# A chunked state recurrence and a wave mixer on one core: each engine's order by a list scheduler in the kernel

## The chip, the cores and the metric

One core of a Trainium2 chip. Its engines run side by side, each in the order of its own queue: TensorE (PE; matmuls, with their weight loads as PEld), VectorE (DVE), ScalarE (ACT), GpSimd (POOL) and SyncE (SP, which only issues DMAs here). TensorE writes to PSUM, which has eight banks. The metric is the device time of a run in microseconds; the profile gives the span from the first to the last instruction of one execution.

## What is computed

Four batches, eight heads, 768 steps, 40 numbers a head. First a recurrence over time for each head, then a mixer over each batch:

```python
for t in range(S):
    y[:, :, t] = np.einsum('bhd,bhde->bhe', rt, state)
    Sa = np.einsum('bhde,bhe->bhd', state, at)
    state_decay = state * wt[:, :, None, :] - np.einsum('bhd,bhe->bhde', Sa, bt)
    state = state_decay + np.einsum('bhd,bhe->bhde', vt, kt)
...
theta = x @ w_theta
zr, zi = x * np.cos(theta), x * np.sin(theta)
u = x + np.einsum('ts,bsd->btd', w_tok_r, zr) + np.einsum('ts,bsd->btd', w_tok_i, zi)
out = u + np.maximum(u @ w_ch, 0.0)
```

Here x is y with the heads side by side, 320 numbers a step.

## The kernel before

The 768 steps are cut into six chunks of 128, so there are 24 tiles (four batches of six), each with 128 steps on the partitions and 320 columns. Tile i is worked on in these steps, which are functions of the kernel:

- load: six DMAs of SyncE bring w, k, b, a, r and v into four sets of raw buffers.
- prep_ln, prep_csi, prep_cse: the log of w (lw, ScalarE), two prefix sums of it as matmuls with triangular matrices, and an exp of each (invW and Wi, two ScalarE instructions). GpSimd multiplies k, b and a by them (kb, ah), and prep_rv casts r and v (rv).
- tr_kb, tr_a, tr_rv: transposes on TensorE against the identity, and copies of the transposed blocks out of PSUM (kbT by VectorE, aT by ScalarE, rvT by whichever evac names).
- sc_psiphi, ev_phi, sc_lams: four sets of score matmuls a tile, 64 rows each, and four masks on VectorE (psi, phi, lamv, lamu). Each set fills two banks.
- rec_x0 gives nx (ScalarE, with its sign turned), rec_nu the solve: nx is brought back through a matmul with the identity, and eight matmuls on phi are added. rec_gt makes the next state gt, rec_gd its transpose.
- out_nut, out_y, out_xt: the read-out y, which VectorE scales into x, and the transpose of x.
- moe_theta, moe_sines, moe_z: theta by three matmuls, its cosine and sine for three tiles at once (ScalarE has to change its function table before and after), and the products zr and zi on GpSimd.
- moe_y, moe_ut, moe_ch: a mixer row of a finished batch, that is twelve matmuls of 320 columns with the token weights, u, its transpose, three matmuls with the channel weights, and the store. wtok_load and wtok_trans bring and turn the token weights, a block of two loads and twelve transposes for each of six; a row needs all six chunks of its batch.

The order around all this is written by hand: one loop over tiles in which solve i stands with the preparation of tiles i + 1 to i + 3, out_y(i - 1) and the mixer rows of rows_at: one row in each of the iterations 9 to 20, two in 21 to 23, and the last batch's six behind the loop. PSUM is two pairs of banks for scores (ps_sc) and four single banks for the rest (ps_sm), handed out in turn. The calls that tc.keep_in_program_order marks keep their place on their engine.

Of the kernel before, what the change touches and what calls it, by code (L numbers as in the profile page):

```python
# [14 lines left out]
LN_EXP = "natural_log_exp_and_others"  # L15


@with_exitstack
def kernel(
# [14 lines left out]
    nc = tc.nc  # L34
# [5 lines left out]
    NT = NCH  # L40
    assert (B, H, S, D) == (4, 8, 768, 40)

    consts = ctx.enter_context(tc.tile_pool(name="consts", bufs=1))
    ident = consts.tile([128, 128], BF16, name="ident")
    make_identity(nc, ident)
    mask_p = consts.tile([128, 1, 128], BF16, name="mask_p")
    make_upper_triangular(nc, mask_p[:, 0, :], 1.0, diag=False)
    mask_n = consts.tile([128, 1, 128], BF16, name="mask_n")
    make_upper_triangular(nc, mask_n[:, 0, :], -1.0, diag=False)
    ntri_inc = consts.tile([128, 128], BF16, name="ntri_inc")  # L50
    make_upper_triangular(nc, ntri_inc, -1.0, diag=True)
# [10 lines left out]
    NB = 4  # L62

    def padded(name, shape, n, pads):
        ts = [consts.tile(shape, BF16, name=f"{name}_{i}") for i in range(n)]
        for i, t in enumerate(ts):
            to_zero.append((i, pads(t)))
        return ts

    to_zero = []  # L70

    def last24(t):
        return t[:, :, D:64] if len(t.shape) == 3 else t[:, :, :, D:64]

    lw_t = padded("lw", [128, H, 64], 2, last24)
    ah_t = padded("ah", [128, H, 64], 2, last24)
    kb_t = padded("kb", [128, 2, H, 64], NB, last24)
    rv_t = padded("rv", [128, 2, H, 64], NB, last24)
    nu_t = padded("nu", [128, H, 64], 2, last24)
    gt_t = padded("gt", [128, G, 2, 64], 2, last24)  # L80
    x_t = padded("x", [128, 3 * 128], 2 * NCH, lambda t: t[:, DM:])
    u_t = padded("u", [128, 3 * 128], 3, lambda t: t[:, DM:])
    for i, t in sorted(to_zero, key=lambda e: e[0]):
        nc.vector.memset(t, 0.0)

    raw = ctx.enter_context(tc.tile_pool(name="raw", bufs=4))
    exps = ctx.enter_context(tc.tile_pool(name="exps", bufs=4))
    trs = ctx.enter_context(tc.tile_pool(name="trs", bufs=3))
    scs = ctx.enter_context(tc.tile_pool(name="scs", bufs=2))
    sml = ctx.enter_context(tc.tile_pool(name="sml", bufs=2))  # L90
    xp = ctx.enter_context(tc.tile_pool(name="xp", bufs=2))
    mw = ctx.enter_context(tc.tile_pool(name="mw", bufs=1))
    mk = ctx.enter_context(tc.tile_pool(name="mk", bufs=2))
    mk1 = ctx.enter_context(tc.tile_pool(name="mk1", bufs=1))
    ps_sc = ctx.enter_context(tc.tile_pool(name="ps_sc", bufs=2, space=PSUM))
# [544 lines left out]
```

## Time and profile before

| | |
|---|---|
| three timed runs | 240.96, 242.19, 242.77 us |
| median | 242.19 us |
| span of the profiled execution | 239.3 us |
| busy: TensorE, VectorE | 205.4, 188.4 us |
| busy: ScalarE, GpSimd | 156.6, 119.2 us |

No separate time is given for the profiled execution; its span stands 2.9 us below the median of the runs, which also take in what lies around the span. TensorE's matmuls overlap, so a piece's duration is longer than the time by which it holds the next one back; that is read from the starts.

### The profile page before, as it was taken

What the parts mean: (1) busy time and instruction counts of PE and PEld (TensorE: products, weight loads), DVE (VectorE), ACT (ScalarE), POOL (GpSimd) and SP (SyncE); (2) the same over time, 40 slices, a digit from 0 to 9 for tenths busy, and PEclk for the clock granted to TensorE, in tenths of its full rate; (3) what the DMA queues carried; (4) which work ended last, traced back from release to release, by engine and by line L of the source; (5) the groups of instructions that cost most, each with busy time, mean ns of one, the idle gap of its engine ahead of it and who ended that gap; (6) DMA issues with size and microseconds to landing.
All of it is one profiled execution on the core that took longest, in us unless ns stands there. A gap on an engine that the chain in (4) does not pass through costs nothing.

```text
span 239.3 us, 8103 instructions
## 1 busy us (share of the span) xinstructions
PE 205.4 (86%) x3368; PEld 161.6 (68%) x3368; DVE 188.4 (79%) x290; ACT 156.6 (65%) x300; POOL 119.2 (50%) x184
## 2 busy tenths in 40 slices
PE   2679698957877999979999999999999998889982
PEld 1467577746655787767787787777777877666740
DVE  7558698895979798988899798979898869645062
ACT  4466577799469956867678785987698648325230
POOL 3009654666957693618753771657464730704100
PEclk9999999999999999999999999999999999999997
DMA  7999999999999999998899999948000000111013
GB/s 125 184 182 146 177 177 152 176 159 189 176 168 183 194 171 160 175 188 145 156 188 179 183 184 167 183 69 151 30 32 4 30 27 3 55 58 55 3 55 110
DMA packets 155684, 30.81 MB, mean 129 GB/s; under 512 B 150400, under 2 KB 155648, under 8 KB 155648
## 3 DMA queue, kind: packets, MB, share of 16 engines
q1 hardware_dynamic: 153216, 27.54, 62.9%
q0 software_dynamic: 2432, 2.77, 8.1%
q8 instruction: 26, 0.43, 0.8%
q14 instruction: 10, 0.08, 0.1%
HBM read 29.13 MB, written 3.93 MB: 138 GB/s over the span
## 4 chain that ended last, share of the span: by engine, by line
PE 50%; ACT 17%; DMA 12%; DVE 11%; issue 7%; POOL 1%; SPq 1%; DVEq 0%; ACTq 0%
PE sm L469 12%; PE sm L196 9%; DMA raw_w<-in_w_dram 9%; PE sc L228 8%; PE sm L424 5%; ACT cs L459 4%; DVE lamu L236 4%; DVE lamv L236 2%; ACT L459 2%; PE sc L469 2%; PE sm L363 2%; ACT lw L139 2%; ACT rvT L104 2%; PE sm L376 2%; DMA raw_a<-in_a_dram 2%
## 5 line engine op out<-in xcount | busy, mean ns | idle before, releaser
L168 POOL TENSOR_TENSOR kb<-raw_kb,invW 128x320 bf16<-128x320 f32 x44 | 37.1, 865 | 69.4 <-ACT invW L163 66.7
L236 DVE TENSOR_TENSOR lamv<-sc,mask_p 128x1024 bf16<-128x1024 f32 x24 | 29.4, 1224 | 12.0 <-PE sc L228 12.0
L469 PE MATMUL sm<-zr,wtok_r 128*128 128x320 bf16 x120 | 33.1, 299 | 0.6 <-DVE gt L324 0.6
L236 DVE TENSOR_TENSOR psi<-sc,mask_p 128x1024 bf16<-128x1024 f32 x24 | 29.3, 1223 | 5.1 <-PE sc L228 4.7
L469 PE MATMUL sm<-zi,wtok_i 128*128 128x320 bf16 x120 | 33.1, 299 | 0.0
L447 POOL TENSOR_TENSOR zr<-cs,x 128x320 bf16<-128x320 f32 x22 | 17.8, 811 | 27.4 <-ACT cs L459 27.3
L236 DVE TENSOR_TENSOR lamu<-sc,mask_p 128x1024 bf16<-128x1024 f32 x24 | 29.2, 1215 | 0.3 <-PE sc L228 0.3
L236 DVE TENSOR_TENSOR phi<-sc,mask_n 128x1024 bf16<-128x1024 f32 x24 | 29.1, 1215 | 0.0
L438 ACT COPY th<-sm 128x320 f32<-128x320 f32 x24 | 10.2, 426 | 18.3 <-PE sm L424 18.2
L345 ACT COPY nuT<-sm 128x512 bf16<-128x512 bf16 x24 | 14.1, 587 | 10.6 <-PE sm L196 10.6
L447 POOL TENSOR_TENSOR zi<-cs,x 128x320 bf16<-128x320 f32 x24 | 19.0, 794 | 3.4 <-ACT cs L459 2.8
L190 POOL TENSOR_TENSOR ah<-raw_a,Wi 128x320 bf16<-128x320 f32 x22 | 19.0, 864 | 0.0
L104 ACT COPY rvT<-sm 128x1024 bf16<-128x1024 bf16 x17 | 17.2, 1014 | 2.3 <-PE sm L196 2.3
L149 POOL CAST rv<-raw_rv 128x320 bf16<-128x320 f32 x44 | 18.6, 451 | 0.0
L477 DVE TENSOR_TENSOR u<-sm,x 128x320 bf16<-128x320 f32 x20 | 9.8, 490 | 10.7 <-PE sm L469 10.7
L469 PEld LDWEIGHTS <-wtok_i 128*128 128x128 bf16 x144 | 14.1, 98 | 6.2 <-issue 0.8
L469 PEld LDWEIGHTS <-wtok_r 128*128 128x128 bf16 x144 | 14.1, 98 | 6.0 <-issue 0.8
L196 PE MATMUL sm<-ident,kb 128*128 128x128 bf16 x192 | 15.7, 227 | 2.5 <-ACT nx L287 1.0
L207 DVE COPY kbT<-sm 128x1024 bf16<-128x1024 bf16 x24 | 16.4, 682 | 1.8 <-PE sm L196 1.8
L196 PE MATMUL sm<-ident,rv 128*128 128x128 bf16 x192 | 15.6, 226 | 1.5 <-ACT invW L163 0.8
L360 PE MATMUL sm<-kb,lamv 128*128 128x40 bf16 x192 | 16.7, 180 | 0.0
L228 PE MATMUL sc<-aT,kbT 64*128 64x128 bf16 x384 | 15.7, 225 | 0.7 <-ACT aT L214 0.7
(111 smaller groups left out, 598.9 us busy)
## 6 DMA issues: line engine op xcount, KB each, us to landing
raw_w<-in_w_dram SPq DMA_DIRECT2D x24, 160.0 KB, 4.1
raw_kb<-in_k_dram SPq DMA_DIRECT2D x24, 160.0 KB, 3.9
raw_kb<-in_b_dram SPq DMA_DIRECT2D x24, 160.0 KB, 4.0
raw_a<-in_a_dram SPq DMA_DIRECT2D x24, 160.0 KB, 3.9
raw_rv<-in_r_dram SPq DMA_DIRECT2D x24, 160.0 KB, 3.8
raw_rv<-in_v_dram SPq DMA_DIRECT2D x24, 160.0 KB, 4.2
out_dram<-oo SPq DMA_DIRECT2D x24, 160.0 KB, 1.8
wtok_row_r<-in_moe_w_tok_r_dram POOLq DMA_DIRECT2D x6, 192.0 KB, 4.2
```

The costliest lines, as they stand in the source:

```text
L104: nc.scalar.copy(out=out, in_=in_)
L149: on_pool(nc.gpsimd.tensor_copy(out=q.rvb[:, j, :, 0:D], in_=q.rv[:, j]))
L168: on_pool((nc.vector if i < 2 else nc.gpsimd).tensor_tensor(out=q.kbh[:, j, :, 0:D], in0=q.kb[:, j], in1=q.invW[:, 0], op=ALU.mult), i)
L190: on_pool((nc.vector if i < 2 else nc.gpsimd).tensor_tensor(out=q.ah[:, :, 0:D], in0=q.a, in1=q.Wi[:, 0:DM].rearrange("p (h d) -> p h d", ...
L196: nc.tensor.transpose(out=dst[:, g * 128:(g + 1) * 128], in_=src[:, 2 * g:2 * g + 2, :].rearrange("p a b -> p (a b)"), identity=ident)
L207: nc.vector.tensor_copy(out=q.kbT.rearrange("p a b -> p (a b)"), in_=pt)
L228: nc.tensor.matmul(P[:, p, g, :], lhsT=lhs[rows(p), g * 128:(g + 1) * 128], rhs=rhs[rows(p), g * 128:(g + 1) * 128], start=True, stop=True)
L236: nc.vector.tensor_tensor(out=s.rearrange("p a b c -> p (a b) c"), in0=P.rearrange("p a b c -> p (a b) c"), in1=mask.to_broadcast([128, 2 ...
L360: nc.tensor.matmul(o, lhsT=q.lamv[:, p, g, :], rhs=q.kbh[:, 0, h, 0:D], start=first, stop=False, skip_group_check=True)
L447: tc.keep_in_program_order(eng.tensor_tensor(out=zs[bi][c][:, js[m]], in0=cs[:, c, m], in1=tiles[bi * NCH + js[m]].x, op=ALU.mult))
L459: tc.keep_in_program_order(nc.scalar.activation(out=cs[:, c, 0:n], in_=ths[bi][:, j0:j0 + n], func=AF.Sin, bias=(pi2_col[:, :], 0.0)[c]))
L469: nc.tensor.matmul(yp, lhsT=wtok[nm][:, sb, j * 128:(j + 1) * 128], rhs=z[:, sb], start=start and n == 0, stop=stop and n == 2 * len(sbs) - 1)
```

## The change

All steps are now described to a planner (class Plan): each with its engine, what it reads and writes, a cost in ns and a priority from a table (OFF, in us, plus PERIOD times the tile). Plan.order simulates the engines, DMA queues and PSUM banks with these costs, and at each point gives an engine the step with the lowest priority, plus a price for time that it would wait. The steps are then issued in the planned order, with no reordering behind it, in the banks that the plan chose: four banks as two pairs, four single. Beside the order these things change:

- The solve adds phi's matmuls to the bank in which x0 still stands. nx is copied without the sign, which moves to the copy of nu; the matmul with the identity is gone.
- Both prefix sums go to one pair of banks, and one exp reads both; four masks and this exp now share the two pairs. off_diag is added to the first sum too, eight columns more.
- Copies of transposed blocks read the 16-bit pairs as 32-bit words, half as many elements, all on ScalarE (those of the token weights stay on VectorE).
- A mixer row is planned in six chunks of two matmuls. Its first chunk takes a bank only if more than two single banks are free (one in the last batch).
- The sines of a batch come as two groups of three, as before, and the last batch's as three, two and one. The last tile's sines read PSUM.

```diff
-    rows_at = {}
-    for s in range(NCH + 3, 3 * NCH + 3):
-        rows_at[s] = [divmod(s - NCH - 3, NCH)]
...
+OFF = dict(load=-32.72, ln=-14.21, cs=-14.27, exp=-12.91, kb=-24.2, ah=-17.45, rv=-8.81,
...
+PERIOD = 7.54
...
+        def find(o):
+            n = o.new[1]
+            if n == 2:
+                c = [(max(bank_free[b], bank_free[b + 1]), (b, b + 1))
+                     for b in range(0, DOUBLE, 2)
+                     if not bank_held[b] and not bank_held[b + 1]]
+                return min(c) if c else None
+            c = [(bank_free[b], (b,)) for b in range(DOUBLE, BANKS) if not bank_held[b]]
+            return min(c) if len(c) > o.spare else None
...
+                for t, o, b in cand:
+                    s = o.prio + wait * (t - lo)
+                    if e == "ACT" and o.table is not None and o.table != table:
+                        s += tswitch
+                    if best is None or (s, o.idx) < best[0]:
+                        best = ((s, o.idx), t, o, b)
...
+    def copy_words(out, in_):
+        nc.scalar.copy(out=out.bitcast(FP32), in_=in_)
...
+        add("ACT", "exp", i, lambda: nc.scalar.activation(
+            out=ex, in_=ps(pk)[:, :, 0:328], func=AF.Exp), 740, [pk], [kex], table="lnexp")
...
-        nps = tile_of(ps_sm, [128, 512], FP32, "sm")
-        nc.tensor.matmul(nps[:, 0:DM], lhsT=ident, rhs=q.nx, start=True, stop=False,
-                         skip_group_check=True)
...
+        def nu_mm():
+            t = ps(pk)
+            for h in range(H):
+                nc.tensor.matmul(t[:, h * D:h * D + D], lhsT=phi[:, h % 2, h // 2, :],
+                                 rhs=nx[:, h * D:h * D + D], start=False, stop=True,
+                                 skip_group_check=True)
...
+            add("PE", "row", q, chunk, 2 * mm(320), need, [pk], pr=base,
+                new=(pk, 1) if n == 0 else None, spare=(2 if bi < B - 1 else 1),
+                loose=bi == B - 1, tail=tail(320))
...
+            add("POOL", "wdma", i, lambda row=row, ap=ap: nc.gpsimd.dma_start(
+                out=row, in_=ap[tb * 128:(tb + 1) * 128, :]), 890, [],
+                [("wrow", nm, tb % 2)], work=1100)
...
+    order = plan.order()
+    table = "lnexp"
+    for o in order:
+        if o.table is not None and o.table != table:
+            table = o.table
+            if table == "lnexp":
+                nc.scalar.preload_act_table_set(LN_EXP)
+        o.fn()
```

What moves is seen in three places. The first is the start of GpSimd's queue, behind the masks. wth and wch are the channel weights, wtok_row or wrow the rows of the token weights, kb, ah and rv the products and casts of tile 2, the first on this engine. Before:

```order
L168 TENSOR_TENSOR kb_92<-raw_kb,invW 128x8x40 x2
L190 TENSOR_TENSOR ah_88<-raw_a,Wi 128x8x40
L149 CAST rv_96<-raw_rv 128x8x40 x2
L389 DMA wth<-in_moe_w_theta_dram 128x2x320
L389 DMA wth<-in_moe_w_theta_dram 64x320
L389 DMA wch<-in_moe_w_ch_dram 128x2x320
L389 DMA wch<-in_moe_w_ch_dram 64x320
```

The four loads of channel weights stood behind tile 2's work, and the first block of token weights behind that of tile 5. Now:

```order
L701 DMA wth<-in_moe_w_theta_dram 128x2x320
L704 DMA wth<-in_moe_w_theta_dram 64x320
L701 DMA wch<-in_moe_w_ch_dram 128x2x320
L704 DMA wch<-in_moe_w_ch_dram 64x320
L712 DMA wrow_r_227<-in_moe_w_tok_r_dram 128x768
L712 DMA wrow_i_229<-in_moe_w_tok_i_dram 128x768
L712 DMA wrow_r_228<-in_moe_w_tok_r_dram 128x768
L712 DMA wrow_i_230<-in_moe_w_tok_i_dram 128x768
L436 TENSOR_TENSOR kb_115<-raw_kb_74,ex_184 128x8x40 x2
L440 TENSOR_TENSOR ah_112<-raw_a_70,ex_184 128x8x40
L445 CAST rv_119<-raw_rv_78 128x8x40 x2
```

The channel weights and two blocks stand ahead of all work, and one load of the third follows behind tile 2's.

The second place is TensorE around the last solve, that of tile 23. psi belongs to x0, phi to the solve. Before:

```order
L283 MATMUL sm<-rv_97,psi 128x40
L283 LDWEIGHTS psi
L283 MATMUL sm<-rv_97,psi 128x40
L292 LDWEIGHTS ident
L292 MATMUL sm<-nx,ident 128x320
L295 LDWEIGHTS phi
L295 MATMUL sm<-nx,phi 128x40
L295 LDWEIGHTS phi
```

Now, with zr and zi in matmuls of a mixer row, and xT and wth in those of theta of tile 22:

```order
L671 LDWEIGHTS wtok_r
L671 MATMUL ps_s_233<-zr_221,wtok_r 128x320
L671 LDWEIGHTS wtok_i
L671 MATMUL ps_s_233<-zi_223,wtok_i 128x320
L520 LDWEIGHTS phi_201
L520 MATMUL ps_s_236<-nx_207,phi_201 128x40
...
L616 LDWEIGHTS xT_211
L616 MATMUL ps_s_235<-wth,xT_211 128x320
L616 LDWEIGHTS xT_211
L616 MATMUL ps_s_235<-wth,xT_211 128x320
```

The identity is gone, two matmuls of a mixer row stand ahead of the solve, and theta of tile 22 right behind it. Along the whole engine the first mixer row now stands behind the solve of tile 7, where it was tile 9, and rows come in pieces between other steps; ahead of tile 7's solve stand the transposes of rv, kb and ah of tile 8. The scores stand in 68 unbroken blocks of 64-row matmuls, where there were 51. Ahead of tile 23's solve stand sixteen rows, as before, and two matmuls; behind it 94 row matmuls.

The third place is ScalarE behind the same solve. th is theta (of tile 22), cs its cosine and sine with tile 21's, uT transposes of the mixer. Before:

```order
L287 ACTIVATE nx<-sm 128x320
L299 CAST nu_99<-sm 128x8x40
L345 COPY nuT<-sm 128x512
L104 COPY xT_5115<-sm 128x384
L438 COPY th<-sm 128x320
L104 COPY uT<-sm 128x384 x2
L459 ACTIVATE cs<-th,pi_col 128x640
L459 ACTIVATE cs<-th 128x640
```

Now:

```order
L514 CAST nx_207<-ps_s_236 128x320
L383 COPY xT_211<-ps_s_235 128x192
L524 ACTIVATE nu_122<-ps_s_236 128x8x40
L626 COPY th_218<-ps_s_235 128x320
L640 ACTIVATE cs_220<-th_218,pi_col 128x640
L640 ACTIVATE cs_220<-th_218 128x640
L383 COPY nuT_197<-ps_s_234 128x256
L383 COPY uT_213<-ps_s_235 128x192
```

theta and its sines have moved ahead of nuT and uT.

## Rows read from the trace of the kernel before

**Rows 1.** The page: busy time by engine, and the DMA engines' tenths in 40 slices.
```profile
PE 205.4 (86%) x3368; PEld 161.6 (68%) x3368; DVE 188.4 (79%) x290; ACT 156.6 (65%) x300; POOL 119.2 (50%) x184
...
DMA  7999999999999999998899999948000000111013
```

**Rows 2.** Three stretches, cut at the solves of tiles 7 and 23.
```profile
core 0: us, PE busy (x) PEld busy (x) DVE busy (x) ACT busy (x) POOL busy (x), PEclk, DMA share, GB/s
0.00:69.00 69.00, 50.93 (x903) 40.97 (x904) 53.18 (x98) 45.48 (x92) 35.12 (x64) 1.00 1.02 168
69.00:208.74 139.74, 130.55 (x2245) 104.74 (x2243) 122.12 (x167) 102.25 (x191) 80.73 (x117) 1.00 0.69 126
208.74:239.30 30.56, 23.96 (x223) 15.86 (x222) 13.07 (x27) 8.82 (x18) 3.39 (x4) 0.96 0.15 55
```

**Rows 3.** Timeline of SyncE's queue: start us, us, what it issues.
```profile
0.74 0.43 SPq L133 DMA_DIRECT2D raw_w<-in_w_dram  x1
...
52.66 1.85 SPq L133 DMA_DIRECT2D raw_w<-in_w_dram  x1
...
59.59 0.72 SPq L133 DMA_DIRECT2D raw_w<-in_w_dram  x1
...
68.33 0.66 SPq L133 DMA_DIRECT2D raw_w<-in_w_dram  x1
```

**Rows 4.** The page's DMA queues: q1 is SyncE's, q0 GpSimd's.
```profile
q1 hardware_dynamic: 153216, 27.54, 62.9%
q0 software_dynamic: 2432, 2.77, 8.1%
```

**Rows 5.** Timeline of TensorE, one tile in the second stretch.
```profile
145.03 0.40 PE L196 MATMUL sm<-ident,gt 128*128 128x128 bf16 x4
...
146.00 0.61 PE L196 MATMUL sm<-ident,kb 128*128 128x128 bf16 x8
146.67 0.30 PE L292 MATMUL sm<-nx,ident 128*128 128x320 bf16 x1
...
147.04 0.18 PE L360 MATMUL sm<-kb,lamv 128*128 128x40 bf16 x1
147.33 0.19 PE L363 MATMUL sm<-kb,lamu 128*128 128x40 bf16 x1
...
149.68 0.61 PE L196 MATMUL sm<-ident,rv 128*128 128x128 bf16 x8
150.13 0.57 PE L424 MATMUL sm<-wch,uT 128*128 128x320 bf16 x3
150.53 0.30 PE L469 MATMUL sm<-zr,wtok_r 128*128 128x320 bf16 x1
...
152.16 0.57 PE L424 MATMUL sm<-wth,xT 128*128 128x320 bf16 x3
152.67 0.40 PE L228 MATMUL sc<-rvT 64*128 64x128 bf16 x8
...
153.22 0.40 PE L196 MATMUL sm<-ident,gt 128*128 128x128 bf16 x4
```

**Rows 6.** Groups by line and shape: busy us, mean ns, idle before.
```profile
L236 DVE TENSOR_TENSOR lamv<-sc,mask_p 128x1024 bf16<-128x1024 f32 x24 | 29.4, 1224 | 12.0 <-PE sc L228 12.0
...
L207 DVE COPY kbT<-sm 128x1024 bf16<-128x1024 bf16 x24 | 16.4, 682 | 1.8 <-PE sm L196 1.8
...
L438 ACT COPY th<-sm 128x320 f32<-128x320 f32 x24 | 10.2, 426 | 18.3 <-PE sm L424 18.2
...
L459 ACT ACTIVATE cs<-th 128x960 f32<-128x960 f32 x7 | 6.9, 987 | 0.0
```

**Rows 7.** Timelines of ScalarE and VectorE, last stretch.
```profile
215.89 0.42 ACT L438 COPY th<-sm 128x320 f32<-128x320 f32 x1 [4.00 <-PE sm L424]
...
217.24 0.84 ACT L459 ACTIVATE cs<-th,pi_col 128x640 f32<-128x640 f32 x1
...
236.11 0.49 DVE L493 SCALAR_TENSOR_TENSOR oo<-sm,u 128x320 f32<-128x320 f32 x1 [0.69 <-DMA out_dram<-oo]
```

More of the change, by code (lines that the diff above doesn't have):

```diff
@@ L87 @@
[L87 to L94, printed above, removed]
@@ L420, with prio, add, pair @@
-    out_r = out.rearrange("b (n p) d -> b n p d", p=128)
+    def prio(kind, i):
+        return 1000.0 * (PERIOD * i + OFF[kind])
+    def add(eng, kind, i, fn, cost, reads=(), writes=(), pr=None, **kw):
+        return plan.add(eng, kind, i, fn, cost, tuple(reads), tuple(writes),
+                        prio(kind, i) if pr is None else pr, **kw)
+    def pair(t, g):
+        return t[:, 2 * g:2 * g + 2, :].rearrange("p a b -> p (a b)")
+    def transpose_pairs(dst, srcs):
+        for j, src in enumerate(srcs):
+            for g in range(G):
+                c = (j * G + g) * 128
+                nc.tensor.transpose(out=dst[:, c:c + 128], in_=pair(src, g), identity=ident)
@@ new lines, in scores, with go @@
+    def scores(i, kind, kindm, lhs, rhs, keys, dst, dkey, mask):
+        p = ("ps", kind, i)
+        def go():
+            t = ps(p).rearrange("p a (g c) -> p a g c", g=G)
+            for g in range(G):
+                for q in range(2):
+                    nc.tensor.matmul(t[:, q, g, :],
+                                     lhsT=lhs[rows(q), g * 128:(g + 1) * 128],
+                                     rhs=rhs[rows(q), g * 128:(g + 1) * 128],
+                                     start=True, stop=True)
+        add("PE", kind, i, go, 8 * 28, keys, [p], new=(p, 2), mode=64, tail=tail(128))
+        add("DVE", kindm, i, lambda: nc.vector.tensor_tensor(
+            out=dst.rearrange("p a b c -> p (a b) c"),
+            in0=ps(p).rearrange("p a (g c) -> p (a g) c", c=128),
+            in1=mask.to_broadcast([128, 2 * G, 128]), op=ALU.mult), 1222, [p], [dkey])
@@ L531, with mix_rows @@
+    def mix_rows(bi):
+        for j in range(NT):
+            mix_row(bi, j)
+    for i in range(3):
+        loads(i)
+    prep(0)
+    attention_scores(0)
+    loads(3)
+    mixer_weights()
     for i in range(N):
         bi, ci = divmod(i, NCH)
-        yrows = rows_at.get(i, [])
-        sines = ci == 4 or (ci == 1 and bi > 0)
-        nxt(load, i + 4)
-        rec_x0(i)
-        nxt(tr_a, i + 1)
-        nxt(tr_kb, i + 1)
-        rec_nu(i)
-        if i > 0:
-            out_y(i - 1)
-        nxt(prep_csi, i + 2)
@@ new lines @@
+        if i + 4 < N:
+            loads(i + 4)
+        recurrence(i)
+        readout(i)
+        theta(i)
+        if i < NT:
+            wtok_block(i)
+        if bi < B - 1:
+            if ci == NCH - 1:
+                sines(bi, (0, 1, 2))
+                sines(bi, (3, 4, 5))
+        elif ci == 2:
+            sines(bi, (0, 1, 2))
+        elif ci == 4:
+            sines(bi, (3, 4))
+        elif ci == 5:
+            sines(bi, (5,))
+        if ci == NCH - 1:
+            mix_rows(bi)
```

973 lines of the change are left out of this document (532 added, 441 removed).

## The prediction

> **What bounds the kernel now.** I read the page first for the busy time of each engine, then the trace cut into three stretches at the solve (the matmuls on nx) of tile 7 and of tile 23, then the load queue, then one tile of TensorE's timeline.
>
> The page names TensorE the busiest engine, at 205.4 us, and the DMA engines as full for the first 60% of the span and nearly empty behind [rows 1]. So there are at least two stages with different limits, and the cut shows them [rows 2]. Stretch A, 0 to 69.00 us: DMA share 1.02, TensorE busy 50.93 of 69 us. Stretch B, 69.00 to 208.74: DMA share 0.69, TensorE busy 130.55 of 139.74, VectorE 122.12, ScalarE 102.25. Stretch C, the last 30.56 us: DMA 0.15, TensorE 23.96, no engine full.
>
> In A SyncE never rests: the first w load goes out at 0.74, that of tile 8 at 52.66, of tile 9 at 59.59, of tile 10 at 68.33 [rows 3]. Tile 9's load is thus 58.85 us behind tile 0's. GpSimd's DMA queue took 8.1% of the engines' span, 19.4 us of all sixteen [rows 4]; by bytes some 2.9 of that are the two channel weights and 2.75 each of the six token-weight blocks (a block is two row loads). By 59.59 the channel weights and two blocks were in, 8.4 us, so nine tiles took 58.85 - 8.4 = 50.4, or 5.6 us a tile. A is a stage of data, not of orders.
>
> For B I take one tile, from one transpose of gt at 145.03 to the next at 153.22: 8.19 us [rows 5]. The starts of the pieces tell what TensorE really needs, since a piece's duration includes a tail that the next one hides. Twelve mixer matmuls take 150.53 to 152.16, 0.136 us each; eight transposes 149.68 to 150.13, 0.056 each. Two holes are seen: behind the eight transposes at 146.00 the next piece could start at 146.45 and starts at 146.67 (0.22), and in the read-out the matmul behind the one at 147.04 could start at 147.07 and starts at 147.33 (0.26). So a tile with one mixer row is 8.19 - 0.48 = 7.71 us of issue, and B's sixteen of them, with the 72 transposes of the token weights (4.0), are 127.4 of its 139.7 us. TensorE stands empty for only 12.3 us in B, although it looks 93% busy or 91% issued; that is all that a better order can win there.
>
> **The change part by part.**
>
> *Arithmetic.* The copy of nx through the identity goes: 146.67 to the phi matmuls is one 320-column pitch, 0.136 us, sixteen times in B, -2.2. Eight columns of off_diag are added once a tile, some 0.025 each, +0.4. The kbT copy leaves VectorE (0.682 x 24 = 16.4 us) for ScalarE, and every transposed block is copied as half as many 32-bit words. No row has a 256- or 512-word copy; 320 words take 426 ns and 960 take 987 as a sine without a bias column [rows 6], so 512 words are an estimated 0.59 us on their line. The bounds are this and twice it, if a word cost what two elements do; I take the line, since both its rows are of 32-bit elements. The other copies that change get shorter or stay, by the same line. Either way both engines are below TensorE in B, 102 and 122 us of 140: I cost it at nothing, covered by TensorE's 127. If TensorE dropped under 122 that cover would be gone, and VectorE's 16 us less would be what counts.
>
> *Array modes.* The score matmuls load 64 rows, all others 128. Three matmuls of 320 columns take 0.40 before another full-array piece (150.13 to 150.53) and 0.51 before scores (152.16 to 152.67): about 0.1 per change of mode [rows 5]. The order of before has 51 blocks of scores, the planned one 68: 17 more, by share 11 of them in B, two changes each, +2.1 us. It cancels the identity copy. The Trainium skill, TensorEngine Tiling (Array Packing), section Key Properties, says that changing the mode drains TensorE, which speaks against splitting the blocks; it gives no figure, and by these rows the trace agrees at 0.1 a change.
>
> *B as a whole.* Of the token-weight transposes only one and a half blocks are left behind tile 7's solve: -3.0. Work in B becomes 127.4 - 2.2 + 0.4 + 2.1 - 3.0 = 124.7. How much of the 12.3 us of holes the order fills no row tells. The bounds are 1% (the mixer's row now comes in pairs of matmuls that can fill any hole, and the first row stands behind tile 7 instead of tile 9) and all 12.3 as now. I take 4%, 5.3 us, because the two holes read above wait for a VectorE mask and for nx, both known to a planner with right durations: B = 130, bounds 126 to 137.
>
> *A.* The order moves all weights forward on GpSimd: the channel weights and two blocks are issued before its first product, where now the channel weights follow the products of tile 2 and the first block those of tile 5. By tile 8, whose v the solve of tile 7 now needs behind it in TensorE's order, five blocks instead of two are ahead or beside. Nine tiles at 5.6 are 50.4, channel weights 2.9, five blocks between 1.8 (59.59 to 68.33 is 8.74, against 6.93 without a block) and 2.75 each: 62 to 67, plus some 4 for the first issue, the landing and the cast: 66 to 71. I take 69.5, nearer to the upper end, since 2.75 is from the queue's own row, so A gains nothing: it is bound by bytes that stay the same, and the shorter run-ahead of TensorE's order (cs of tile i+1 ahead of solve i, where now ScalarE's in-order Ln of tile i+3 stands ahead) pays for the weights.
>
> *C.* Now theta of tile 22 stands behind two whole rows, and ScalarE copies it at 215.89 and starts the sines at 217.24 [rows 7], 8.5 us after the solve; the order puts theta right behind the solve. Left from there on TensorE: 94 row matmuls 12.8, ten sets of three at 0.40, 4.0, nine sets of three transposes 1.5, transposes of nu, scores and read-out 1.1: 19.4. The last add starts at 236.11, 3.2 before the end [rows 7], and the copy of uT and the matmuls' tail before it add 0.8; holes for the last sines 1.0. C = 24.5, bounds 22.5 to 27, against 30.56 [rows 2].
>
> Sum: 69.5 + 130 + 24.5 = 224.0 us of span. The span of the profiled run is 239.3 and the median of the three timed runs 242.19, 2.9 more; I add the same: 226.9, rounded to **226**. Runs of this kernel lie 0.8% apart, so 1% is about what can be told from no change.
>
> **Rivals.**
> 1. *Denser than I say.* Holes of 1% in B, and blocks that cost 1.8 each: 66.5 + 126 + 23.5 + 2.9 = 219. For it: rows in pairs fill any hole. Against: only four single banks, and a row may take one only while others stay free.
> 2. *Weights first.* If a block takes its whole 2.75 us and the sixth also gets ahead, tile 8 lands at 50.4 + 19.4 + 3 = 72.8 and the solve of tile 7 is at 74.5: 74.5 + 130 + 24.5 + 2.9 = 232. For it: GpSimd's packets are long, 19.4 us x 16 engines over 2432 is 128 ns, a load's 16 [rows 4]; taken in turns, loads would get one part in nine while weights wait. The Trainium skill, DMA: Bandwidth & Descriptors, section Queues, rings and completion order, says just that each engine takes packets from its queues in turn. Against: total bytes are the same, and A was full anyway.
> 3. *The order is no denser than now.* 12.3 us of holes stay: 69.5 + 137 + 27 + 2.9 = 236.
> 4. *Slower: bank pairs.* One exp over both prefix sums needs a bank pair, so five users a tile share two pairs where four did; each score frees its pair only after a mask of 1.224 us on VectorE [rows 6]. With a fixed order TensorE stands when its next pair is late. At 0.4 a time, 2 us a tile, B is 125 + 32 = 157 and the run 254. It decides from where B passes 145.3 (C gains 6), 20.6 us of holes, 0.26 a user. Against: five tenancies of about 1.7 (0.45 of matmuls and the mask) are 8.5 of two pairs' 15.4 us.
>
> **How the numbers follow.** Forecast 0.56, rival 1 0.14, rival 2 0.13, rival 3 0.09, rival 4 0.08. The first three are faster by over 1%, and most of the fourth: 0.86. Rival 4 is 0.08, and 0.06 is left for no change. The range runs from 217, below rival 1, to 238, above rival 3; what it leaves out is rival 4 and ends beyond rival 1's own.
>
> **What would show it.** Solve of tile 7 at 66 to 72 us, and DMA share near 1 up to there; the first mixer row right behind it, not two tiles later; from solve 7 to solve 23 some 130 us, 16 tiles of 8.1; VectorE's busy time down by at least the 16.4 of kbT and ScalarE's not up; 24.5 us from the last solve to the end. It is wrong if tile 7's solve comes after 75, or if TensorE waits for masks or bank pairs over 0.26 us a score in B.

## The result, and the profile after

The changed kernel takes 221.84 us (median of runs from 220.93 to 222.87), against 241.57 for the kernel before beside it: ratio 0.9198, 95% interval 0.9128 to 0.9268. The profiled execution took 221.09 us with a span of 219.2. The forecast was 226, the range 217 to 238.

First the page, busy time by engine and the DMA engines' tenths, which answers [rows 1].

```profile
PE 198.0 (90%) x3368; PEld 155.4 (71%) x3368; DVE 167.2 (76%) x250; ACT 147.1 (67%) x319; POOL 119.2 (54%) x184
...
DMA  6999999999999899999999999999980000100121
```

TensorE lost 7.4 us of busy time, VectorE 21.2, ScalarE 9.5, GpSimd none, while the span lost 20.1. So most of the gain is time in which TensorE had stood idle. The same three stretches as in [rows 2], cut at the solves of tiles 7 and 23:

```profile
core 0: us, PE busy (x) PEld busy (x) DVE busy (x) ACT busy (x) POOL busy (x), PEclk, DMA share, GB/s
0.00:71.36 71.36, 54.12 (x974) 43.52 (x975) 52.84 (x101) 45.24 (x96) 39.95 (x71) 1.00 1.03 171
71.36:194.50 123.14, 123.05 (x2205) 97.83 (x2204) 102.59 (x128) 95.57 (x208) 76.18 (x110) 1.00 0.76 139
194.50:219.20 24.70, 20.80 (x193) 14.05 (x191) 11.74 (x22) 6.28 (x16) 3.05 (x4) 1.00 0.17 60
```

The first is 2.4 us longer than before, the second 16.6 shorter, the last 5.9 shorter: 20.1 in all. In the second, TensorE is now busy 123.05 of 123.14 us, and the view of TensorE's waits has no row at all for it.

What goes on in the first stretch is seen in SyncE's queue (start, duration, what it issues), which answers [rows 3]. The rows are the w loads of tiles 0, 1, 2, 8 and 9:

```profile
0.74 0.44 SPq L398 DMA_DIRECT2D raw_w<-in_w_dram  x1
...
6.03 1.64 SPq L398 DMA_DIRECT2D raw_w<-in_w_dram  x1
...
16.70 1.08 SPq L398 DMA_DIRECT2D raw_w<-in_w_dram  x1
...
56.56 0.63 SPq L398 DMA_DIRECT2D raw_w<-in_w_dram  x1
...
67.25 0.73 SPq L398 DMA_DIRECT2D raw_w<-in_w_dram  x1
```

Tile 2's goes out at 16.70 and tile 9's at 67.25, where it was 59.59. Ahead of tile 2's load stand GpSimd's loads of the channel weights and of the first two blocks, of which these are the first and the last of eight:

```profile
2.78 0.90 POOL L701 DMA_DIRECT2D wth<-in_moe_w_theta_dram  x1
...
8.42 0.59 POOL L712 DMA_DIRECT2D wrow_i<-in_moe_w_tok_i_dram  x1
```

TensorE's timeline tells how long it stands at the start; the time in brackets is how long it stood before the piece, and for what:

```profile
10.56 1.04 PE L380 MATMUL ps_s<-ident,rv 128*128 128x128 bf16 x8
16.02 0.42 PE L414 MATMUL ps_d<-lw,ntri_inc 128*128 128x320 bf16 x1 [4.42 <-ACT lw L407]
```

The log of tile 1's w (lw) comes late, at 15.50 where it came at 11.33 before, and TensorE stands from the end of tile 0's transposes to 16.02. That the loads ahead are the reason is tried in e3.

One tile of TensorE in the second stretch, to be read beside [rows 5]:

```profile
142.52 0.17 PE L424 MATMUL ps_d<-off_diag,ident 128*128 128x8 bf16 x1
142.54 0.36 PE L520 MATMUL ps_s<-nx,phi 128*128 128x40 bf16 x8
142.75 0.57 PE L616 MATMUL ps_s<-wch,uT 128*128 128x320 bf16 x3
143.15 0.30 PE L671 MATMUL ps_s<-zr,wtok_r 128*128 128x320 bf16 x1
143.29 0.30 PE L671 MATMUL ps_s<-zi,wtok_i 128*128 128x320 bf16 x1
143.43 0.40 PE L380 MATMUL ps_s<-ident,nu 128*128 128x128 bf16 x4
...
146.96 0.66 PE L380 MATMUL ps_s<-ident,kb 128*128 128x128 bf16 x8
147.45 0.20 PE L593 MATMUL ps_s<-gd,rvT 128*128 128x80 bf16 x1
147.49 0.18 PE L600 MATMUL ps_s<-kb,lamv 128*128 128x40 bf16 x1
147.56 0.19 PE L602 MATMUL ps_s<-kb,lamu 128*128 128x40 bf16 x1
```

The two holes of [rows 5] are gone. The solve is followed by other work, the channel matmuls and a pair of row matmuls (0.136 a matmul), before nu's transposes are wanted; behind the eight transposes at 146.96 the next piece starts at 147.45, 0.49 later, just their pitch with 0.04 to spare; and the read-out on lamu at 147.56 comes 0.07 behind the one on lamv at 147.49, where it was 0.29.

The groups of ScalarE's copies, which answer [rows 6] (busy us, mean ns, idle before):

```profile
L383 ACT COPY rvT<-ps_s 128x512 f32<-128x512 f32 x24 | 14.2, 590 | 9.2 <-PE ps_s L380 9.0
L383 ACT COPY uT<-ps_s 128x192 f32<-128x192 f32 x24 | 7.7, 320 | 17.4 <-PE ps_s L572 13.9
L429 ACT ACTIVATE ex<-ps_d 128x656 f32<-128x656 f32 x24 | 17.2, 718 | 2.9 <-PE ps_d L424 2.0
L383 ACT COPY kbT<-ps_s 128x512 f32<-128x512 f32 x24 | 14.0, 584 | 7.5 <-PE ps_s L380 7.1
```

And the last stretch, ScalarE's theta and first sines, then VectorE's last add, which answers [rows 7]:

```profile
195.31 0.43 ACT L626 COPY th<-ps_s 128x320 f32<-128x320 f32 x1
195.83 0.83 ACT L640 ACTIVATE cs<-th,pi_col 128x640 f32<-128x640 f32 x1
...
216.03 0.49 DVE L691 SCALAR_TENSOR_TENSOR oo<-ps_s,u 128x320 f32<-128x320 f32 x1 [1.12 <-PE ps_s L616]
```

Theta is copied 0.8 us behind the solve at 194.50 instead of some 7, and the last add starts 3.2 us before the end, as it did before.

To compare kernels I sum the middle stretch from the starts of all TensorE pieces in it. Each piece is charged the pitch at which such pieces follow one another [rows 5] (0.136 us for 320 columns, 0.056 for 128, 0.025 at least), each change of array mode 0.09, and what is left between two starts is a hole. The planner's end time is what Plan.order computes from its own costs. Kernels ran beside different runs of before, so ratios are what compares them. The medians of e2 and e14 take in one and two runs of a slower state, without which they are 232.81 and 226.00 (the ratios leave such runs out), and e14's stretches are left out because its profiled execution was one of them. Times are in us.

A hole in this sum need not be a wait. In the middle stretch the granted clock stood at the lower of its two levels (1.2 GHz) for 3.4 us in e3, e8 and e12 and for 6.8 us in e6; by the starts some 1.4 us of each 3.4 are counted as holes for it. In the first stretch it stood there for 10.2 us in e1, 6.8 in e3 and e7 and 3.4 in e13. Before and after had it at the upper level in both stretches.

| kernel | median | ratio, 95% interval | solve 7 at | middle | work | mode | holes | planner's end |
|---|---|---|---|---|---|---|---|---|
| before | 241.57 | | 69.0 | 139.7 | 115.3 | 5.8 | 18.6 | |
| after | 221.84 | 0.9198 [0.9128, 0.9268] | 71.4 | 123.1 | 111.6 | 7.6 | 3.9 | 210.8 |
| e1, hand order, new arithmetic | 243.48 | 1.0062 [1.0028, 1.0095] | 70.9 | 140.6 | 113.7 | 6.2 | 20.7 | |
| e2, planner, old arithmetic | 233.22 | 0.9615 [0.9565, 0.9666] | 74.4 | 131.4 | 115.0 | 8.4 | 8.0 | 220.2 |
| e12, e2 with a table of its own | 228.18 | 0.9426 [0.9389, 0.9462] | 71.6 | 129.1 | 113.5 | 7.6 | 8.0 | 214.0 |
| e7, planner, only 16-bit copies | 234.62 | 0.9730 [0.9680, 0.9781] | 76.9 | 133.6 | 113.9 | 8.2 | 11.5 | 221.0 |
| e14, e7 with a table of its own | 227.78 | 0.9381 [0.9323, 0.9439] | | | | | | 213.7 |
| e10, after's order, 16-bit copies | 238.38 | 0.9847 [0.9813, 0.9881] | 77.0 | 134.8 | 111.7 | 7.6 | 15.5 | |
| e4, more TensorE | 233.24 | 0.9673 [0.9629, 0.9717] | 74.0 | 133.3 | 122.9 | 7.6 | 2.8 | |
| e5, more VectorE | 228.41 | 0.9479 [0.9433, 0.9525] | 72.7 | 129.3 | 111.8 | 7.6 | 9.8 | |
| e3, weights late | 227.69 | 0.9367 [0.9287, 0.9447] | 69.9 | 130.8 | 113.2 | 7.1 | 10.5 | 209.9 |
| e6, mask booked at half | 247.50 | 1.0229 [1.0161, 1.0297] | 76.0 | 146.4 | 113.4 | 7.6 | 25.4 | 212.9 |
| e8, mode changes dear | 242.59 | 1.0058 [1.0026, 1.0090] | 74.6 | 141.7 | 112.5 | 6.0 | 23.1 | 231.7 |
| e13, after, new table | 221.68 | 0.9161 [0.9130, 0.9193] | 72.8 | 123.1 | 111.3 | 6.7 | 5.1 | 208.3 |

### The profile page after: what moved, and what is told of

It reads as the page before. It is cut to its first block, busy times and chain, and to the rows that moved or that the text cites. A ratio compares the mean times of both kernels' runs of the same rounds, so it can differ in the third digit from the quotient of the medians.

```text
span 219.2 us, 8154 instructions
## 1 busy us (share of the span) xinstructions
PE 198.0 (90%) x3368; PEld 155.4 (71%) x3368; DVE 167.2 (76%) x250; ACT 147.1 (67%) x319; POOL 119.2 (54%) x184
## 4 chain that ended last, share of the span: by engine, by line
PE 74%; DMA 7%; DVE 6%; POOL 3%; ACT 3%; issue 3%; SPq 2%; DVEq 0%; ACTq 0%; POOLq 0%
PE ps_s L671 18%; PE ps_s L380 15%; PE ps_d L468 11%; PE ps_s L616 9%; DMA raw_w<-in_w_dram 7%; PE ps_s L572 4%; PE ps_s L538 2%; PE ps_s L520 2%; SPq L398 2%; PE ps_s L602 2%; PE ps_s L508 2%; DVE lamu L473 2%; PE ps_s L600 2%; DVE psi L473 2%; PE ps_s L502 1%
## 5 line engine op out<-in xcount | busy, mean ns | idle before, releaser
L436 POOL TENSOR_TENSOR kb<-raw_kb,ex 128x320 bf16<-128x320 f32 x44 | 37.1, 863 | 49.7 <-ACT ex L429 49.1
L671 PE MATMUL ps_s<-zr,wtok_r 128*128 128x320 bf16 x144 | 40.8, 300 | 0.0
L671 PE MATMUL ps_s<-zi,wtok_i 128*128 128x320 bf16 x144 | 40.7, 299 | 0.0
L473 DVE TENSOR_TENSOR lamu<-ps_d,mask_p 128x1024 bf16<-128x1024 f32 x24 | 29.3, 1221 | 5.3 <-PE ps_d L468 4.6
L473 DVE TENSOR_TENSOR psi<-ps_d,mask_p 128x1024 bf16<-128x1024 f32 x24 | 29.2, 1216 | 5.3 <-PE ps_d L468 5.3
L473 DVE TENSOR_TENSOR lamv<-ps_d,mask_p 128x1024 bf16<-128x1024 f32 x24 | 29.2, 1218 | 5.0 <-PE ps_d L468 2.7
L473 DVE TENSOR_TENSOR phi<-ps_d,mask_n 128x1024 bf16<-128x1024 f32 x24 | 29.3, 1219 | 1.9 <-PE ps_d L468 1.6
L652 POOL TENSOR_TENSOR zr<-cs,x 128x320 bf16<-128x320 f32 x23 | 17.9, 792 | 10.3 <-ACT cs L640 10.2
L429 ACT ACTIVATE ex<-ps_d 128x656 f32<-128x656 f32 x24 | 17.2, 718 | 2.9 <-PE ps_d L424 2.0
L440 POOL TENSOR_TENSOR ah<-raw_a,ex 128x320 bf16<-128x320 f32 x22 | 19.0, 866 | 0.0
L468 PE MATMUL ps_d<-aT,kbT 64*128 64x128 bf16 x384 | 18.3, 223 | 0.7 <-ACT aT L383 0.5
```

The lines of the kernel that those rows point to most:

```text
L429: add("ACT", "exp", i, lambda: nc.scalar.activation(out=ex, in_=ps(pk)[:, :, 0:328], func=AF.Exp), 740, [pk], [kex], table="lnexp")
L436: lambda j=j: (nc.vector if fast else nc.gpsimd).tensor_tensor(out=kb[:, j, :, 0:D], in0=raw_kb[s4][:, j], in1=invW, op=ALU.mult),
L440: lambda: (nc.vector if fast else nc.gpsimd).tensor_tensor(out=ah[:, :, 0:D], in0=raw_a[s4], in1=Wi, op=ALU.mult),
L468: nc.tensor.matmul(t[:, q, g, :], lhsT=lhs[rows(q), g * 128:(g + 1) * 128], rhs=rhs[rows(q), g * 128:(g + 1) * 128], start=True, stop=True)
L473: add("DVE", kindm, i, lambda: nc.vector.tensor_tensor(out=dst.rearrange("p a b c -> p (a b) c"), in0=ps(p).rearrange("p a (g c) -> p (a g ...
L652: nc.vector if fast else nc.gpsimd).tensor_tensor(
```

## The experiments

My theory was that TensorE bounds the middle and the order closes its holes, while the first stretch is bound by the loads and the arithmetic is worth little by itself. The rivals were that the arithmetic carries the gain, that weights issued first cost the first stretch, and that VectorE or ScalarE became the bound.

**e1: the arithmetic alone.** The kernel before with its hand-written order, the solve in place, and the transposed copies as words on ScalarE.

```diff
-            nc.vector.tensor_copy(out=out, in_=in_)
+        nc.scalar.copy(out=out.bitcast(FP32), in_=in_)
...
-        nc.tensor.matmul(nps[:, 0:DM], lhsT=ident, rhs=q.nx, start=True, stop=False,
+        nps = q.xps
```

> The kernel before, its loop and pools unchanged, with the arithmetic of the change: the solve added in place, all copies of transposed blocks as 32-bit words on ScalarE. Theory one (the order fills TensorE's holes): the identity's 24 x 0.136 = 3.3 us go from TensorE and VectorE's 25 us less are covered, so 237 to 240 us, a span some 2 to 4 below 239.3, with 15 to 18 us of holes still in the stretch between the solves of tiles 7 and 23. Rival (shorter copies close the holes, the order does little): half or more of the 20 us of gain, 232 or less.

Measured: 243.48 us, ratio 1.0062, slower than before, which neither theory had. VectorE's busy time fell from 188.4 to 167.5 and the middle grew by 0.8: work fell by 1.6, holes rose by 2.0. The other 1.9 us of the longer span lie in the first stretch, where the mean granted clock was 0.93 and not 1.00. The two largest of TensorE's waits in the middle (total us, times, longest):

```profile
engine line waited for: us in total, times, longest us
PE sc L225 <- ACT rvT L101: 4.7, 4, 1.3
PE sm L362 <- DVE lamu L233: 1.7, 6, 0.3
```

The scores on rvT now wait for the copy on ScalarE. Copies went to VectorE while ScalarE made sines, and that is what I had taken away. An engine 21 us emptier gave nothing: from before to e1, that view's waits for ScalarE go from 4.4 to 7.8 us, and those for VectorE do not fall (2.8 and 4.5).

**e2: the order with the old solve and copies.** The planner with the identity matmul in a bank of its own, 16-bit copies, and kbT on VectorE, with their durations told to it. The single exp over both prefix sums, the groups of sines and the early weights stay as in the change.

```diff
-                190 + n / 2.4, [psk], writes)
+                160 + n / 1.2, [psk], writes)
...
+            nc.tensor.matmul(t[:, 0:DM], lhsT=ident, rhs=nx, start=True, stop=False,
```

> The change's planner with the arithmetic of before: identity matmul in a bank of its own, 16-bit copies, kbT by VectorE, each at its own cost in the plan. Theory one: TensorE has 0.136 us a tile more, 3.3 in all, the rest is covered: 224 to 227 us. Rival (copies): most of the gain is lost, 232 or more.

Measured: 233.22 us, in the rival's range; the first theory missed. Holes fell from 18.6 to 8.0, but solve 7 came at 74.4, and the gain was less than half of the change's. That looked as if order and arithmetic paid only together, until e12 was run.

**e3: the weights later.** A block's loads may be issued only behind the rv cast of tile 4, 6, 8, 9, 10 or 11, and those of the second channel weight (wch) only behind tile 3's; the two loads of wth stay ahead.

```diff
+    for key, i in {0: 4, 1: 6, 2: 8, 3: 9, 4: 10, 5: 11, 'wch': 3}.items():
+        for o in late[key]:
+            o.pre.append(cast[i])
```

> The change, with GpSimd's loads of token weights held behind the casts of tiles 4, 6, 8, 9, 10, 11 (blocks 0 to 5) and the second channel weight behind tile 3. Theory one (the first stretch is bound by bytes): three blocks of 1.8 to 2.75 us leave it, the solve of tile 7 comes at 63 to 66 us instead of 71.4 and the run ends 5 to 8 us sooner, 214 to 217. Rival A (the first stretch is a chain of waits, not bytes): 221 to 223. Rival B (the weights then come too late for the mixer rows, or the later loads suffer): 224 or more.

Measured: 227.69 us, slower than the change by some 6 us by the medians and 4 by the ratios: rival B, and not my theory. Its stretches, the second cut once more at the solve of tile 11 (columns as above):

```profile
0.00:69.91 69.91, 52.72 (x956) 41.92 (x957) 50.59 (x96) 45.52 (x97) 37.90 (x66) 0.95 0.99 164
69.91:110.11 40.20, 36.17 (x607) 29.18 (x603) 28.66 (x40) 26.21 (x58) 25.36 (x40) 0.96 1.04 172
110.11:200.75 90.64, 90.04 (x1621) 71.61 (x1619) 76.34 (x95) 68.83 (x150) 53.08 (x75) 1.00 0.63 121
```

Solve 7 comes 1.45 us earlier, and then tiles 8 to 11 take 10 us each, with the DMA engines at 1.04 and TensorE busy 36.17 of 40.20. The same four tiles in the change, and in the kernel before:

```profile
71.36:102.96 31.60, 31.58 (x574) 25.34 (x572) 25.94 (x33) 25.63 (x55) 22.06 (x33) 1.00 0.99 167
69.00:104.95 35.95, 31.33 (x571) 25.44 (x569) 32.71 (x46) 26.38 (x49) 23.03 (x34) 1.00 1.07 178
```

So e3 loses 8.6 us on the change in these four tiles and gains 0.9 behind them. By the sum of the starts 6.0 of them are holes (7.2 against 1.2; 1.4 of it is the lower clock) and 2.5 work, of which 1.7 are 30 transposes of token weights that the change has behind it by then. GpSimd's waits from 69.9 to 118 us name the loads:

```profile
POOL kb L436 <- ACT ex L429: 9.9, 3, 6.1
POOL rv L445 <- DMA raw_rv<-in_r_dram: 5.0, 2, 4.4
POOL rv L445 <- DMA raw_rv<-in_v_dram: 3.7, 3, 2.6
```

These are 18.6 us, where the same waits in the change (71.4 to 118) are 14.3; TensorE waits 3.9 us in e3's four tiles, 2.1 of them for kb from GpSimd, and in the change it has no wait there.

At the start the edit does what it should. ScalarE turns tile 1's w at

```profile
10.77 0.47 ACT L407 ACTIVATE lw<-raw_w 128x320 bf16<-128x320 f32 x1
```

where the change has it at 15.50, and the solve of tile 0 comes at 13.94 instead of 17.97. But these 4 us have shrunk to 1.45 by tile 7 (how much of that is the clock, 0.95 in this stretch, is not shown), and the same bytes then stand in the way of tiles 8 to 11, where TensorE has other work to do. In the change TensorE stands early, and from the solve of tile 7 on hardly at all. The kernel before brought its token weights late too, issued from 42 to 85 us, and had 7.8 of its 18.6 us of holes in these four tiles. So up to 6.6 of the 14.7 us of holes that the change closes, those of these four tiles, may be due to the place of the weights on GpSimd's queue and not to TensorE's own order; no run moves the weights alone in the order of before.

**e4 and e5: who bounds the middle.** In after's own order, more work that the planner does not know of: five matmuls of 320 columns a tile for TensorE,

```diff
+            for _ in range(5):
+                nc.tensor.matmul(t[:, 0:DM], lhsT=ident, rhs=vb[:, :, 0:D], start=True,
+                                 stop=True, skip_group_check=True)
```

and half a mask a tile for VectorE:

```diff
+            if kindm == "mphi":
+                nc.vector.tensor_tensor(
+                    out=extra, in0=ps(p)[:, 0].rearrange("p (g c) -> p g c", c=128),
```

> The changed kernel's order as it is, with five more matmuls of 320 columns in each tile ahead of the x0 matmuls, which nothing reads (their result is overwritten); at the pitch of such matmuls in the trace of after that is an estimated 0.68 us of TensorE a tile, and the planner does not know of it. Theory one, TensorE is the bound from the solve of tile 7 to that of tile 23 (123.05 of 123.14 us busy) and the loads before it: the 16 tiles of the middle stretch grow by 16 x 0.68 = 10.9 us and the first stretch by little, so 231 to 234 us in all. Rival, the busy time of TensorE is only filled by an early start and the bound is the chain through VectorE and ScalarE: under 4 us more, at most 226.

> The changed kernel's order as it is, with half a mask more on VectorE in each tile right behind the mask of the phi scores (an estimated 0.69 us, half of the 1.22 that a whole mask takes and its fixed part), which nothing reads and the planner does not know of. Theory one, TensorE is the bound and VectorE has room (102.59 of 123.14 us busy in the middle stretch): 222 to 226 us. Rival, the order is tight enough that what VectorE hands over late becomes a hole of TensorE each time, as where the planner booked masks at half: the 16 tiles of the middle stretch grow by up to 11 us, 229 or more.

Measured: 233.24 and 228.41 us. The middle stretch of e4, then that of e5, e5's group of the added instruction, and TensorE's largest wait in e5's middle:

```profile
74.04:207.37 133.33, 133.21 (x2288) 106.02 (x2285) 103.00 (x128) 95.74 (x208) 75.08 (x109) 1.00 0.69 127
```

```profile
72.73:202.00 129.27, 125.18 (x2206) 98.61 (x2204) 110.86 (x143) 95.70 (x208) 75.57 (x109) 1.00 0.71 131
```

```profile
L480 DVE TENSOR_TENSOR extra<-ps_d,mask_n 128x512 bf16<-128x512 f32 x24 | 16.3, 680 | 0.0
```

```profile
PE ps_d L415 <- DVE extra L480: 2.3, 8, 0.4
```

With e4 the middle grows by 10.2 us for 10.9 added, and the first stretch by 2.7 for 5.4: TensorE is the bound of the middle, as theory one had it, and in the loads' stretch half of the added work shows. e5 fell between its two theories. VectorE stands idle for 18 of 129 us, yet 16 x 0.68 = 10.9 us added there cost 6.1, nearly all of it holes of TensorE (3.9 to 9.8). The added instruction reads the scores and so holds their bank pair 0.68 us longer; the wait shown is TensorE's for a pair to be free. Room in an engine's sum is not room at the place where the order needs it.

**e6: a wrong duration.** The planner is told 611 ns for a mask instead of 1222; nothing else changes.

```diff
-            in1=mask.to_broadcast([128, 2 * G, 128]), op=ALU.mult), 1222, [p], [dkey])
+            in1=mask.to_broadcast([128, 2 * G, 128]), op=ALU.mult), 611, [p], [dkey])
```

> The change, with a mask booked in the plan at 611 ns instead of 1222; what runs is the same, only the order differs. Theory one (the order closes holes because its durations are right): TensorE now waits for masks and bank pairs, 5 to 15 us slower than the change, 227 to 237. Rival (any order that runs ahead far enough and weaves the mixer rows in does it): within 2 us of the change.

Measured: 247.5 us, slower than before and far over what I expected, with 25.4 us of holes. TensorE's waits in the middle:

```profile
PE ps_s L602 <- DVE lamu L473: 4.1, 9, 0.7
PE ps_s L380 <- DVE gt L546: 3.8, 6, 1.1
PE ps_d L468 <- DVE psi L473: 1.9, 2, 1.3
```

The read-out on lamu and the scores wait for masks, the transposes of gt for gt, which VectorE makes. My fourth rival had drawn such a picture for the change itself, with waits for bank pairs alone; here those (ps_d behind psi, phi and lamv) are 4.1 of the 14.3 us that the view lists. The run is 26 us longer than the change. A part of that may be that the table was not made for these durations, as in e2, and some 2.9 us of the holes are the lower clock.

**e7: 16-bit copies, solve in place.** As e2, without the identity matmul and its bank.

```diff
-        nc.scalar.copy(out=out.bitcast(FP32), in_=in_)
+        nc.scalar.copy(out=out, in_=in_.bitcast(BF16))
```

> The changed kernel's planner and its solve in place, but transposed blocks copied as 16-bit elements again (kb's on VectorE), with their longer times told to the planner. Between the order with both old parts (233.2) and the whole change (221.8) lie 11.4 us. Theory one, the identity matmul and its bank are the smaller part (an estimated 3.6 us of TensorE from 24 matmuls of 320 columns) and the copies, which TensorE waits for, the larger: 227 to 231 us. Rival, the in-place solve is nearly all of it, since TensorE is the bound and the copies are beside it: 221 to 225.

Measured: 234.62 us, over both ranges and no better than e2, though it has less to do. So the distance of e2 and e7 from the change was not a price of their arithmetic alone.

**e8: longer runs of one mode.** The planner's choice is charged 16 us for a change of mode.

```diff
+                    if e == "PE" and o.mode != mode:
+                        s += 16000
```

> The changed kernel, where the planner books 16 us for each change of the TensorE array's mode when it chooses what comes next, so that transposes and plain matmuls stand in fewer and longer runs (53 separate score blocks instead of 68 or more). Theory one, mode changes cost the 7.6 us in the middle stretch that I summed from the starts and some of it comes back: 219 to 221.5 us. Rival, the clusters make VectorE and ScalarE wait in turn: 223 or more.

Measured: 242.59 us. Mode changes fell from 7.6 to 6.0 us, holes rose from 3.9 to 23.1. The rival held, and stronger than I put it: in this order, with a table not made for it, longer runs of one mode open far more holes than they save in changes at 0.09 each. The planner's own end time had said so before, 231.7 against 210.8. The Trainium skill, TensorEngine Tiling (Array Packing), section Key Properties, says that a change of mode drains TensorE; the trace agrees, with that 0.09 us a change, but avoiding changes cost twelve times what it saved.

**e10: after's order, slower copies.** The order is kept to the instruction; only the copies read 16-bit elements (the edit of e7's copies, with kbT left on ScalarE and without telling the planner).

> The changed kernel with its order kept to the instruction (the planner is told the old short durations), but the transposed blocks copied as 16-bit elements by ScalarE. By the rows of before and after a copy of 1024 elements then takes 1014 ns instead of 590 for its 512 words, one of 512 elements 587 ns, one of 384 elements 487 instead of 320: an estimated 1.7 us more of ScalarE a tile, whose busy time would go from 147 to about 188 us of the span. Theory one, in this order TensorE waits for whatever is late by more than it was planned (half a mask more on VectorE gave back 6.6 of 16.6 us as waits): 230 to 240 us. Rival, ScalarE is busy 95.6 of 123.1 us in the middle stretch and has room: at most 226.

Measured: 238.38 us, theory one. The groups of the two largest copies and the middle stretch:

```profile
L383 ACT COPY rvT<-ps_s 128x1024 bf16<-128x1024 bf16 x24 | 24.6, 1025 | 7.4 <-PE ps_s L380 7.4
L383 ACT COPY kbT<-ps_s 128x1024 bf16<-128x1024 bf16 x24 | 24.5, 1019 | 5.8 <-PE ps_s L380 5.7
```

```profile
77.00:211.84 134.84, 128.45 (x2206) 99.70 (x2204) 103.31 (x128) 118.17 (x208) 74.78 (x109) 1.00 0.67 123
```

TensorE's work is the same 111.7 us, and its holes go from 3.9 to 15.5, with ScalarE busy 118.17 of 134.84 us. In this order the short copies are worth some 16 us.

**e12 and e13: new tables.** The priorities (with PERIOD and the two constants that place the mixer rows) and the planner's prices for waiting and for a change of ScalarE's table were searched anew, by random steps that kept whatever shortened the planner's own end time; for the old arithmetic (e12, from e2) and for the change itself (e13). Of e13's edit, the last lines:

```diff
-PERIOD = 7.54
-ROWLAG = 7.44
-ROWSTEP = 7.6
+PERIOD = 7.3990
+ROWLAG = 6.42
+ROWSTEP = 7.51
```

> The planner with both old parts of the arithmetic (identity matmul in a bank of its own, 16-bit copies, kb's on VectorE), as in the run that gave 233.2 us, but with the table of priorities (and the planner's two other constants) searched anew for these durations, so that the planner's own end time falls from 220.2 to 214.0; that of the changed kernel is 210.8. Theory one, the table was fitted to the durations of the new arithmetic, which is why the old arithmetic lost 11 us in it, and most of the change's gain can be had by order alone: 224 to 228 us. Rival, order and arithmetic pay only together, whatever the table: 231 or more.

> The changed kernel with nothing but the table of priorities and the planner's two other constants searched anew, from the table that it has: the planner's own end time falls from 210.8 to 208.3. Theory one, the time follows the planner's, and the changed kernel is not at the end of what order gives: 218 to 220.5 us. Rival, what is left is work of TensorE (111.6 of 123.1 us in the middle stretch) and the loads, and the planner's last 2.5 us are inside what its model misses: 221 to 224 us.

Measured: 228.18 and 221.68 us. e12 takes 5 us off e2 with the same instructions, to the upper end (228) of theory one's range and 0.2 over it: the old solve and copies had suffered from a table made for other durations. By the ratios, the order with the old solve and copies gives 5.7%, and the whole change 8.0%. What the single exp and the new groups of sines, which e12 shares with the change, are worth was not tried apart. e13 took the rival's side. The planner's end fell by 2.5 us and the time did not move beyond its interval; the middle is 123.1 us in both.

**e14: which part of the arithmetic.** As e7, with a table searched for its durations, in the same way.

> The planner with the solve in place, but with 16-bit copies (kb's on VectorE), and with its table of priorities and two constants searched anew for these durations; the planner's own end time falls from 221.0 (the run that gave 234.6 us) to 213.7, beside 214.0 for both old parts of the arithmetic with a searched table (228.2 us) and 210.8 for the changed kernel (221.8 us). Theory one, of the 6 us between these two times the copies carry most, since they stand in the chain that TensorE waits for, and the identity matmul only its own time on TensorE (an estimated 2.3 us: 11.4 us of the run with five more such matmuls, by five): 225.5 to 228 us. Rival, the in-place solve carries most, since TensorE is the bound: 222 to 224.5.

Measured: 227.78 us, ratio 0.9381 [0.9323, 0.9439], inside theory one. From e12 to e14, the in-place solve, is 0.45 points, inside the intervals; from e14 to the change, the word copies and kbT on ScalarE, is 1.8 points, some 4.4 us, and the intervals don't meet. A search ends somewhere, so the times of e12 and e14 are upper bounds of what the best order would give.

## Why the prediction was right, and where its sum was off

The direction, the place and most of the mechanism held: TensorE's holes in the middle are what the order closes. The total was 4 us too high (the sum's 226.9 had been put down as 226).

*Middle stretch.* Forecast 130, bounds 126 to 137, measured 123.14: this is the term that failed, by 6.9 us. I had read one tile with 0.48 us of holes, taken the rest, 7.71, for work, and multiplied by sixteen. Summed over all tiles, work and mode changes were 121.1 us of the 139.7 and holes 18.6, not 127.4 and 12.3: the tile I chose was one of the denser ones, with 0.7 us of holes where the mean is 1.2, and a few holes in it were too short to catch my eye. It also had every step, which not all sixteen have, and 60 transposes of token weights lie in the stretch, not 72. Work fell by 1.9 (I said 2.7), to 119.2 where I had 124.7; that is 5.5 of the 6.9. The order closed 14.7 of 18.6 us of holes where I took 7 of 12.3, and left 3.9 where I had 5.3; that is the other 1.4. My reason, that waits for a mask and for nx can be filled by a planner with right durations, is supported by e6, where one wrong duration opens 21 us of holes again (2.9 of them the lower clock, and a part perhaps the table's). It is not all of it: late weights alone (e3) open 6.6 us again, 1.4 of them the clock, and the sum held the weights' place only as a cost of the first stretch. That row pairs are what fills the holes was not tried by itself.

*Arithmetic at nothing.* Right for the order of before (e1: no gain), wrong for the new one: between e12 and the change lie 2.3 points, some 5.5 us, of which the sum had 2.2, the identity. That e12's middle, 129.1, stands beside the forecast's 130 is luck: its work and mode changes are 121.1 and its holes 8.0, where I had 124.7 and 5.3. I argued from busy sums, that ScalarE and VectorE have room below TensorE. e5 and e10 show that in a dense order a longer step costs TensorE in spite of such room. That the shorter copies let a denser order exist is supported by e12 and e14, whose searched tables did not reach the change's time. The durations were right: 590 and 584 ns for 512 words where I had 0.59 us. The Trainium skill, ScalarE: Activation LUTs, section Step-by-step: what each stage is for, states one element a cycle for 32-bit and 16-bit elements alike; the trace agrees, 1025 ns for 1024 16-bit elements in e10 and 590 for the same bytes as words.

*Array modes.* +2.1 us forecast for the middle, +1.8 measured.

*First stretch.* Forecast 69.5, bounds 66 to 71, measured 71.36, with the DMA engines at 1.03: no gain, as said, and 0.4 over the bound. e3 shows that the weights' place is worth 1.45 us at solve 7 and that putting them later costs 4 to 6 in the end. The rival of weights first had the mechanism (e3) at some three times its size, 5 us at solve 7.

*Last stretch.* 24.5 forecast, 24.70 measured: with theta right behind the solve, as reasoned there.

*Bank pairs* (the slower rival). The view lists no wait of TensorE for a mask or a pair in the middle; the exp in the pairs costs nothing that can be seen there.

*Sum.* +1.9, -6.9, +0.2, and 1.9 us instead of 2.9 around the span: 226.9 - 5.8 = 221.1, the profiled execution's own time. Nearest came rival 1, denser than I say, at 219, though with other stretches. Of the chances, 0.83 and most of rival 3's 0.09 are a little more than the 0.86 written.

What stays open: how much of the planner's gain is the rule, how much the table and how much the weights' place. e2 to e12 and e7 to e14 move by 5 to 7 us by the table alone, and the change's table is at an end that e13 could not improve on.

## What to carry to other kernels

Before costing a reorder, sum the bounding engine's holes over the whole stretch from its starts; one tile read closely gave two thirds of them here. A static order is only as good as its durations: a step 0.7 us longer than planned costs the bound engine even where the step's own engine is a seventh idle (e5), so after every change of a step's length the order has to be made anew before old and new are compared. Put transfers that must be made anyway where the bound engine has nothing else to do.

## What the runs showed of the hardware that I had not expected

Weight loads on GpSimd's queue, issued from 2.78 to 8.42 us, held one load of SyncE's queue back by some 4.7 us: tile 1's w is turned at 15.50 with all eight in front and at 10.77 with only the two of wth (e3). The DMA engines' mean share does not tell the two apart, 1.03 in the change's first stretch and 0.99 in e3's. A planner's end time that lay 8 to 13 us under the span in six kernels with right durations (the change, e2, e7, e8, e12, e13) was 15.6 us under it in e3 and 35.1 in e6: in e6 the duration is the cause, with some 2.9 us of lower clock; in e3 up to some 4 us are the lower clock (10.2 us of its first two stretches), which puts the rest beside the other six.

A hole of TensorE may cost twice. In the middle of e3, e6, e8 and e12 TensorE had stood in one wait or two just before the clock fell; in e12 for 1.57 us:

```profile
73.82 0.50 PE L380 MATMUL ps_s<-ident,nu 128*128 128x128 bf16 x4 [1.57 <-ACT nu L528]
74.11 0.47 PE L537 MATMUL ps_s<-gt,ident 128*128 128x320 bf16 x1
74.38 0.27 PE L542 MATMUL ps_s<-rv,kb 128*128 128x80 bf16 x1
```

From 73.98 to 77.39 the granted clock was 0.50, and the matmul of 320 columns held the next one back by 0.27 us instead of 0.136. The change, with no wait listed in its middle, kept a clock of 1.00 there; but so did the kernel before with its holes, so that only this order of events is shown.
